# Lightning attention with a two-layer FFN on one core: step order from a list scheduler, transposes on the DMA queue, decay powers on V and the output

## The chip, the core and the metric

The kernel runs on one NeuronCore of a Trainium2 chip. The metric is the device time of one execution in microseconds (us). The span of a profile is about 1.8 us shorter than the device time of the same execution. A lower time is better. Each version was run several times on one chip, beside the kernel before; the median is given, with the lowest and the highest in brackets. A run is called slow when it is over 1.5% above the fastest of its kernel, and slow runs are left out of all comparisons.

In the profile PE is TensorE (matmul), PEld its weight loads, DVE is VectorE, ACT ScalarE, POOL GpSimd and SP SyncE. The letter q after an engine (SPq, POOLq) means its queue, in which it issues DMAs. L342 is line 342 of the kernel. POOL and GpSimd are the same engine in the text too.

## The reference

An attention with a decay per head is followed by an FFN. B=4, H=8, S=768, D=64; the FFN goes from 512 to 2048 columns and back.

```python
def _attn_ref(q, k, v, lam):                       # cut, and shortened to formulas
    for b in range(nb):                            # blocks of 64 positions
        intra = (q_b @ k_b.T * lam ** (i - j) for i >= j) @ v_b
        inter = (q_b * lam ** (pos + 1)) @ kv_state
        out[:, :, sl] = intra + inter
        kv_state = lam ** 64 * kv_state + (k_b * lam ** (63 - pos)).T @ v_b

def _moe_ref(x, w_in, w_out, alpha):
    h = x @ w_in
    s = np.sin(alpha * h)
    g = h + s * s / (alpha + 1e-09)
    return (g @ w_out).astype(np.float32)
# x = attention output, 3072 tokens x 512
```

## The kernel before

The attention is cut into 24 *units*, numbered 0 to 23. A unit is one batch, four heads and 256 positions, held as 128x512 elements each of Q, K and V. Four units give the input of one *group* of 512 tokens; there are six groups. For a unit the kernel loads Q, K and V (256 KB each), scales them to bf16, transposes Q and K, computes scores, masks them, and multiplies with V. FFN1 (times w_in, then sine and square) makes 16 tiles of 128x512 for a group; FFN2 (times w_out) makes four tiles of 512 columns from 16 matmuls each.

The decay is put into the operands: Q is multiplied by E = lam^pos and K by R = 1/E, V is only cast.

```python
    def scale_q(u, eng):
        ...
        eng.tensor_tensor(out=QL[:], in0=stage[u][0]...,
                          in1=E[:, :, hs].unsqueeze(3).to_broadcast([P, 2, HH, D]), op=ALU.mult)
    def scale_k(u, eng):   # the same with stage[u][1] and R
    def cast_v(u, eng):    # a copy to bf16
    def transposes(u, tag="s0", split=False):        # eight 128x128 transposes on PE
        ...
                    nc.tensor.transpose(out=pts[j][:, hp, par, :],
                                        in_=cast[u, key][:, par, 2 * hp:2 * hp + 2, :],
                                        identity=iden[:])
        ...
            nc.scalar.copy(out=QT[:], in_=pt[:])
```

The order of all instructions on each engine is written by hand. Units 0 to 7 come first, with four filler matmuls of zeros after each; then FFN1 of group 0 and half of FFN1 of group 1; then steps of one kind, called `macro`:

```python
    busy(N0)                                     # 28 filler matmuls
    ...
    group(0, "hps")                              # units 0-3; busy(4) after each
    group(1, "hps")                              # units 4-7; w_in is issued at units 5-7
    ...
    alone(NFC, hook0, (V, A, V, A, G, A, V, G))  # FFN1 of group 0: squares on DVE, ACT, POOL
    alone(NPRE, hook1)                           # 8 tiles of FFN1 of group 1

    def macro(n, nf, mid=None, late=None):
        ...   # scores of unit n, output of unit n-1, state of unit n
        F1 = [ffn1(*f1q.pop(0), V) for _ in range(nf)]   # squares on DVE
        F2 = blocks(ffn2(*f2q.pop(0)), 4)
        for j in range(4):
            st = F1[j] if j < nf else []
            run(st[:-1])
            if j == 1 and n + 1 < NU:
                transposes(n + 1)                # on PE
            run(st[-1:])
            run(F2[j])
            ...
    for n in range(8, NU + 4):
        macro(n, 4 if n >= 12 else NFC // 4 - NPRE // 4, mid2, late2)
```

Of the kernel before, what the change touches and what calls it, by code (L numbers as in the profile page):

```python
# [12 lines left out]
ET = mybir.EngineType  # L14
# [3 lines left out]
def kernel(  # L18
# [24 lines left out]
    RING = 8  # L43
    WIN0 = 5
    GATE = 8
    N0 = 28
    NB = 4
    NPRE = 8
# [3 lines left out]
    wpool = ctx.enter_context(tc.tile_pool(name="wts", bufs=1))  # L52
    stagep = ctx.enter_context(tc.tile_pool(name="stage", bufs=RING))
    work = ctx.enter_context(tc.tile_pool(name="work", bufs=3))
    kvp = ctx.enter_context(tc.tile_pool(name="kv", bufs=2))
    xtp = ctx.enter_context(tc.tile_pool(name="xt", bufs=3))
    gbp = ctx.enter_context(tc.tile_pool(name="gb", bufs=3))
    mlps = ctx.enter_context(tc.tile_pool(name="mlps", bufs=3))
    outp = ctx.enter_context(tc.tile_pool(name="outp", bufs=3))
    PS = bass.MemoryType.PSUM  # L60
    ps = ctx.enter_context(tc.tile_pool(name="ps", bufs=1, space=PS))

    ctx.enter_context(tc.manual_schedule())


# [7 lines left out]
    BUFS = {"s0": 1, "s1": 1, "okv": 1, "hps": 3, "ops": 1}  # L73
    stage = {}

    def load(u, after=None):
        _, tp, b, _, hh = where(u)
        st = []
        for nm, src in (("q", q), ("k", k), ("v", v)):
            tl = stagep.tile([P, HH, 2, D], FP32, name=f"st_{nm}")  # L80
            ld = nc.sync.dma_start(  # L81
                out=tl[:].rearrange("p h two e -> p h (two e)"),
                in_=src[b, hh * HH:(hh + 1) * HH, tp * W:(tp + 1) * W, :]
                .rearrange("h (p two) e -> p h (two e)", two=2))
            if after is not None:
                tc.add_manual_dep(ld.ins, after.ins.name, mybir.DependencyInfo(
                    mybir.DependencyClass.Sync, mybir.DependencyReason.DATA))
                after = None
            st.append(tl)
        stage[u] = st  # L90

    zeros = consts.tile([P, 2 * P], BF16, name="zeros")
    nc.vector.memset(zeros[:], 0.0)
    warm = consts.tile([1, 1], FP32, name="warm")
    nc.vector.memset(warm[:], 0.0)  # L95
    nc.scalar.activation(out=warm[:], in_=warm[:], func=ACTF.Sin)
    lam_bc = consts.tile([P, H], FP32, name="lam_bc")
    nc.sync.dma_start(out=lam_bc[:], in_=lam.partition_broadcast(P))
    alpha_r = consts.tile([NFC, P], FP32, name="alpha_r")
    nc.scalar.dma_start(out=alpha_r[:], in_=moe_alpha.rearrange("(f p) -> f p", p=P))  # L100
    for u in range(8):
        load(u)

# [3 lines left out]
    for c in range(2):  # L107
        sl = slice(c * D, (c + 1) * D)
        nc.gpsimd.iota(out=pos[sl, :], pattern=[[0, 1]], base=1, channel_multiplier=2,
                       allow_small_or_imprecise_dtypes=True)  # L110
        nc.gpsimd.iota(out=jt[sl, :], pattern=[[1, 2]], base=0, channel_multiplier=2,
                       allow_small_or_imprecise_dtypes=True)
    it = consts.tile([P, 2, D], FP32, name="it")
    nc.gpsimd.iota(out=it[:], pattern=[[1, 2], [2, D]], base=0, channel_multiplier=0,
                   allow_small_or_imprecise_dtypes=True)
# [5 lines left out]
    nc.vector.tensor_tensor(  # L121
        out=mask[:], in0=it[:].rearrange("p two e -> p (two e)").unsqueeze(1)
        .to_broadcast([P, 2, 2 * D]),
        in1=jt[:].unsqueeze(2).to_broadcast([P, 2, 2 * D]), op=ALU.is_ge)
    E = consts.tile([P, 2, H], FP32, name="E")
    R = consts.tile([P, 2, H], FP32, name="R")
    nc.gpsimd.tensor_tensor(out=E[:, 0], in0=lam_bc[:], in1=pos[:].to_broadcast([P, H]),
                            op=ALU.pow)

    LT = consts.tile([P, H], FP32, name="LT")  # L130
    nc.vector.tensor_tensor(out=LT[:], in0=lam_bc[:], in1=lam_bc[:], op=ALU.mult)
    for i in range(6):
        nc.vector.tensor_tensor(out=LT[:], in0=LT[:], in1=LT[:], op=ALU.mult)
    nc.vector.tensor_tensor(out=E[:, 1], in0=E[:, 0], in1=lam_bc[:], op=ALU.mult)
    nc.vector.reciprocal(out=R[:], in_=E[:])
# [3 lines left out]
    w_in_sb = wpool.tile([P, NDC, DFF], BF16, name="w_in_sb")  # L139
    w_out_sb = wpool.tile([P, NFC, DM], BF16, name="w_out_sb")  # L140
    WCH = 4

    def load_w_in(j):
        w = DFF // WCH
        nc.gpsimd.dma_start(
            out=w_in_sb[:, :, j * w:(j + 1) * w],
            in_=moe_w_in[:, j * w:(j + 1) * w].rearrange("(c p) g -> p c g", p=P))

    def load_w_out(j):
        n = NFC // WCH  # L150
        nc.gpsimd.dma_start(
            out=w_out_sb[:, j * n:(j + 1) * n, :],
            in_=moe_w_out[j * n * P:(j + 1) * n * P, :].rearrange("(f p) d -> p f d", p=P))

    cast = {}

    def scale_q(u, eng):
        hh = where(u)[4]
        QL = work.tile([P, 2, HH, D], BF16, name="QL")
        hs = slice(hh * HH, (hh + 1) * HH)  # L160
        eng.tensor_tensor(out=QL[:], in0=stage[u][0][:].rearrange("p h two e -> p two h e"),  # L161
                          in1=E[:, :, hs].unsqueeze(3).to_broadcast([P, 2, HH, D]),
                          op=ALU.mult)
        cast[u, "q"] = QL

    def scale_k(u, eng):
        hh = where(u)[4]
        KD = work.tile([P, 2, HH, D], BF16, name="KD", bufs=4)
        hs = slice(hh * HH, (hh + 1) * HH)
        eng.tensor_tensor(out=KD[:], in0=stage[u][1][:].rearrange("p h two e -> p two h e"),  # L170
                          in1=R[:, :, hs].unsqueeze(3).to_broadcast([P, 2, HH, D]),
                          op=ALU.mult)
        cast[u, "k"] = KD

    def cast_v(u, eng):
        VB = work.tile([P, 2, HH, D], BF16, name="VB", bufs=4)
        v_in = stage[u][2][:].rearrange("p h two e -> p two h e")
        if eng is nc.scalar:
            nc.scalar.copy(out=VB[:], in_=v_in)  # L179
        else:  # L180
            eng.tensor_copy(out=VB[:], in_=v_in)
        cast[u, "v"] = VB

    qkt = {}

    def transposes(u, tag="s0", split=False):
        QT = work.tile([P, 2, 2, 2, P], BF16, name="QT")
        if split:
            pts = [ps.tile([P, 2, 2, P], BF16, name="pt", tag=tag, bufs=BUFS[tag])
                   for j in range(2)]  # L190
        else:
            pt = ps.tile([P, 2, 2, 2, P], BF16, name="pt", tag=tag, bufs=BUFS[tag])
            pts = [pt[:, 0], pt[:, 1]]
        for j, key in ((0, "q"), (1, "k")):
            for hp in range(2):
                for par in range(2):
                    nc.tensor.transpose(out=pts[j][:, hp, par, :],  # L197
                                        in_=cast[u, key][:, par, 2 * hp:2 * hp + 2, :],
                                        identity=iden[:])
        if split:  # L200
            nc.scalar.copy(out=QT[:, 1], in_=pts[1][:])  # L201
            nc.vector.tensor_copy(out=QT[:, 0], in_=pts[0][:])
        else:
            nc.scalar.copy(out=QT[:], in_=pt[:])  # L204
# [378 lines left out]
```

## Time and profile before

| | before |
|---|---|
| time in the first runs, before the change was run | 236.38 us, median of 3 (235.03 to 236.7) |
| first FFN1 matmul starts | 31.84 us |
| one steady step (a unit's attention, 4 tiles of FFN1, one of FFN2) | 8.37 us |
| PE idle from the first FFN1 matmul to the last matmul (31.84 to 229.7) | 7.4 us |

The next lines are from the page of the kernel before. Part 2 shows the busy share of each engine in 40 equal slices of the span, in tenths (9 is 90% or more). PEclk is the clock that the throttle granted PE, DMA the share of the DMA engines. Part 4 is the chain of waits: the work that ended last, followed backwards.

```profile
span 234.5 us, 5410 instructions
## 1 busy us (share of the span) xinstructions
PE 213.9 (91%) x2166; PEld 113.9 (49%) x2189; DVE 154.4 (66%) x261; ACT 131.6 (56%) x216; POOL 115.5 (49%) x182
...
PE   8687689968899999999999999999999999998991
...
PEclk9999999997999999999999999999999999999999
...
PE 71%; SPq 7%; DVE 6%; POOL 4%; issue 4%; ACT 4%; DMA 2%; POOLq 0%; ACTq 0%
```

PE is above 90% in nearly all slices from the twelfth on (about 65 us), and it makes 71% of the chain. The gain must come from less work on PE, or from an earlier start.

One steady step is the PE timeline of the kernel before (start us, duration, engine, line, operation, out<-in, form, count). A duration holds the modelled drain of the last matmul, so one reads steps from start to start:

```profile
129.62 1.03 PE L369 MATMUL ops<-w_out_sb,gall 128*128 128x512 bf16 x4
...
131.34 0.39 PE L197 MATMUL pt<-iden,QL 128*128 128x128 bf16 x4
131.57 0.39 PE L197 MATMUL pt<-iden,KD 128*128 128x128 bf16 x4
131.79 1.03 PE L369 MATMUL ops<-w_out_sb,gall 128*128 128x512 bf16 x4
...
137.99 0.81 PE L369 MATMUL ops<-w_out_sb,gall 128*128 128x512 bf16 x3
```

The step takes 137.99 - 129.62 = 8.37 us. The eight transposes of the next unit take 131.79 - 131.34 = 0.45 us of it, with nothing beside them on PE.

The largest single wait of PE after the first units is in the list of PE's waits in the kernel before (who waited, line, for whom: total us, times, longest):

```profile
PE pt L197 <- DVE gall L356: 2.9, 1, 2.9
```

The timelines show its cause. First DVE's, then GpSimd's, of the kernel before:

```profile
48.77 3.40 DVE L355 TENSOR_TENSOR s_1127<-s_1125 128x512 bf16<-128x512 bf16 x1
```

```profile
48.84 1.06 POOL L161 TENSOR_TENSOR QL<-st_q,E 128x512 bf16<-128x512 f32 x1
49.85 1.04 POOL L170 TENSOR_TENSOR KD<-st_k,R 128x512 bf16<-128x512 f32 x1
50.85 1.03 POOL L355 TENSOR_TENSOR s_1153<-s_1151 128x512 bf16<-128x512 bf16 x1
```

One square on DVE took 3.40 us and ended at 52.17 us, 0.3 us after the last of GpSimd's three operations; at 54.19 and 55.30 us, with GpSimd idle, the same square took 0.42 us. This is what the Trainium skill describes in "SBUF — State Buffer", Who interferes with whom: DVE's second read port is GpSimd's port, and it is an exclusive lock. The trace agrees here.

### The profile page before, as it was taken

To read this page: it belongs to the slowest core of one execution; us is meant where nothing else is said; L and a number is where in the kernel's file an instruction comes from. 1 tells how busy PE (TensorE), PEld (TensorE's weight loads), DVE (VectorE), ACT (ScalarE), POOL (GpSimd) and SP (SyncE) were. 2 spreads that over 40 slices of the span, in tenths; PEclk is the share of its full clock that TensorE was granted. 3 is DMA by queue.
4 is the path that set the end of the run, shared out by engine and by line. 5 is a ranking of instruction groups with operands and counts; after the bars stand their busy time and mean duration, and the time that the engine had idled before them with its cause. 6 is when DMAs were issued, how large, how long until landed. Compare 5 with 4: busy or idle time off the path is not lost.

```text
span 234.5 us, 5410 instructions
## 1 busy us (share of the span) xinstructions
PE 213.9 (91%) x2166; PEld 113.9 (49%) x2189; DVE 154.4 (66%) x261; ACT 131.6 (56%) x216; POOL 115.5 (49%) x182
## 2 busy tenths in 40 slices
PE   8687689968899999999999999999999999998991
PEld 5465544324455554555555455455455444443440
DVE  3887948997766556686686687677668756765000
ACT  2466669966755755665646656556565535453110
POOL 5568976980989997855854642651511000000000
PEclk9999999997999999999999999999999999999999
DMA  5999899999846555534633633621122022210333
GB/s 153 296 291 290 148 181 184 207 180 268 236 124 179 155 156 157 150 77 137 178 70 113 180 101 90 173 45 25 22 48 45 0 48 45 45 43 13 82 67 67
DMA packets 46281, 29.72 MB, mean 127 GB/s; under 512 B 2208, under 2 KB 43184, under 8 KB 46256
## 3 DMA queue, kind: packets, MB, share of 16 engines
q1 hardware_dynamic: 42000, 25.18, 41.8%
q0 software_dynamic: 4224, 4.19, 11.8%
q8 instruction: 17, 0.28, 0.5%
q14 instruction: 8, 0.07, 0.1%
q10 hardware_dynamic: 32, 0.01, 0.0%
HBM read 27.28 MB, written 6.29 MB: 143 GB/s over the span
## 4 chain that ended last, share of the span: by engine, by line
PE 71%; SPq 7%; DVE 6%; POOL 4%; issue 4%; ACT 4%; DMA 2%; POOLq 0%; ACTq 0%
PE ops L369 35%; PE hps L342 26%; SPq L81 7%; PE pt L197 3%; PE sp L219 2%; DMA st_k<-in_k_dram 2%; DVE gall L356 2%; PE okv L313 2%; PE okv L298 2%; DVE s_1127 L355 1%; DVE QL L161 1%; ACT xt L324 1%; PE okv L247 1%; ACT ob L376 1%; POOL KD L170 1%
## 5 line engine op out<-in xcount | busy, mean ns | idle before, releaser
L342 PE MATMUL hps<-xt,w_in_sb 128*128 128x512 bf16 x364 | 94.8, 383 | 3.1 <-ACT xt L324 1.2
L369 PE MATMUL ops<-w_out_sb,gall 128*128 128x512 bf16 x381 | 94.6, 379 | 0.9 <-ACT ob L376 0.7
L342 PEld LDWEIGHTS <-w_in_sb 128*128 128x128 bf16 x384 | 36.4, 99 | 44.7 <-issue 4.5
L369 PEld LDWEIGHTS <-gall 128*128 128x128 bf16 x384 | 36.9, 98 | 42.6 <-issue 1.0
L230 DVE TENSOR_TENSOR ST<-sp,mask 128x512 bf16<-128x512 f32 x48 | 30.8, 682 | 1.5 <-PE sp L219 1.2
L170 POOL TENSOR_TENSOR KD<-st_k,R 128x512 bf16<-128x512 f32 x24 | 26.4, 1099 | 5.7 <-DMA st_k<-in_k_dram 5.1
L204 ACT COPY QT<-pt 128x1024 bf16<-128x1024 bf16 x16 | 16.2, 1012 | 21.9 <-PE pt L197 21.9
L376 ACT COPY ob<-ops 128x512 f32<-128x512 f32 x24 | 14.0, 585 | 19.1 <-PE ops L369 19.1
L324 ACT CAST xt<-okv 128x512 bf16<-128x512 f32 x24 | 14.1, 587 | 6.1 <-PE okv L247 5.2
L161 POOL TENSOR_TENSOR QL<-st_q,E 128x512 bf16<-128x512 f32 x16 | 17.4, 1088 | 0.0
L197 PE MATMUL pt<-iden,QL 128*128 128x128 bf16 x96 | 9.6, 223 | 4.8 <-DVE gall L356 2.9
L197 PE MATMUL pt<-iden,KD 128*128 128x128 bf16 x96 | 9.6, 224 | 3.5 <-POOL KD L170 3.4
L197 PEld LDWEIGHTS <-QL 128*128 128x128 bf16 x96 | 6.8, 99 | 9.7 <-issue 4.1
L179 ACT CAST VB<-st_v 128x512 bf16<-128x512 f32 x14 | 8.6, 616 | 5.1 <-DMA st_v<-in_v_dram 5.1
L419 PE MATMUL bz<-zeros 128*128 128x256 bf16 x60 | 10.3, 326 | 1.1 <-DVE warm L95 1.1
L219 PE MATMUL sp<-QT 64*64 64x128 bf16 x384 | 9.9, 221 | 0.7 <-ACT QT L201 0.7
L313 PE MATMUL okv<-ST,VB 64*64 64x128 bf16 x384 | 9.8, 218 | 0.0
L197 PEld LDWEIGHTS <-KD 128*128 128x128 bf16 x96 | 6.3, 100 | 4.7 <-POOL KD L170 4.7
L161 DVE TENSOR_TENSOR QL<-st_q,E 128x512 bf16<-128x512 f32 x8 | 7.8, 970 | 1.0 <-DMA st_q<-in_q_dram 0.9
L419 PEld LDWEIGHTS <-zeros 128*128 128x128 bf16 x60 | 6.5, 117 | 2.7 <-DVE warm L95 1.1
L219 PEld LDWEIGHTS <-QT 64*64 64x64 bf16 x384 | 6.4, 106 | 2.9 <-ACT QT L201 0.8
L247 PE MATMUL okv<-VB,KD 64*64 64x64 bf16 x320 | 7.2, 193 | 0.3
(531 smaller groups left out, 316.5 us busy)
## 6 DMA issues: line engine op xcount, KB each, us to landing
st_q<-in_q_dram SPq DMA_DIRECT2D x24, 256.0 KB, 4.0
st_k<-in_k_dram SPq DMA_DIRECT2D x24, 256.0 KB, 4.6
st_v<-in_v_dram SPq DMA_DIRECT2D x24, 256.0 KB, 5.1
out_dram<-ob SPq DMA_DIRECT2D x48, 128.0 KB, 2.4
w_in_sb<-in_moe_w_in_dram POOLq DMA_DIRECT2D x4, 512.0 KB, 6.5
w_out_sb<-in_moe_w_out_dram POOLq DMA_DIRECT2D x4, 512.0 KB, 8.1
lam_bc<-in_lam_dram SPq DMA_DIRECT2D x1, 4.0 KB, 3.0
alpha_r<-in_moe_alpha_dram ACTq DMA_DIRECT2D x1, 8.0 KB, 2.9
```

The costliest lines, as they stand in the source:

```text
L81: ld = nc.sync.dma_start(out=tl[:].rearrange("p h two e -> p h (two e)"), in_=src[b, hh * HH:(hh + 1) * HH, tp * W:(tp + 1) * W, :] .rearr ...
L161: eng.tensor_tensor(out=QL[:], in0=stage[u][0][:].rearrange("p h two e -> p two h e"), in1=E[:, :, hs].unsqueeze(3).to_broadcast([P, 2, HH ...
L170: eng.tensor_tensor(out=KD[:], in0=stage[u][1][:].rearrange("p h two e -> p two h e"), in1=R[:, :, hs].unsqueeze(3).to_broadcast([P, 2, HH ...
L197: nc.tensor.transpose(out=pts[j][:, hp, par, :], in_=cast[u, key][:, par, 2 * hp:2 * hp + 2, :], identity=iden[:])
L204: nc.scalar.copy(out=QT[:], in_=pt[:])
L219: nc.tensor.matmul(out=sp[hd][half[c], par, hp, :], lhsT=QT[half[hd], 1, hp, par, half[c]], rhs=QT[half[hd], 0, hp, :, half[c]], start=Tru ...
L230: nc.vector.tensor_tensor(out=ST[:, hd], in0=sp[hd][:], in1=mask[:].unsqueeze(2).to_broadcast([P, 2, 2, P]), op=ALU.mult)
L324: nc.scalar.copy(out=xt[g][:, 2 * hh:2 * hh + 2, bb, :, :].rearrange("p hp c i -> p c hp i"), in_=okv[:, :, 0:2 * P].rearrange("p c (hp i) ...
L342: f1mm[g, f] = nc.tensor.matmul(out=hps, lhsT=w_in_sb[:, c, f * P:(f + 1) * P], rhs=xt[g][:, c].rearrange("p b c i -> p (b c i)"), start=( ...
L369: f2mm[:] = [nc.tensor.matmul(out=ops[:], lhsT=gall[g][:, f, m * P:(m + 1) * P], rhs=w_out_sb[:, f, :], start=(f == 0), stop=(f == NFC - 1))]
L376: nc.scalar.copy(out=ob[:], in_=ops[:])
L419: nc.tensor.matmul(out=bz[:], lhsT=zeros[:, :P], rhs=zeros[:], start=True, stop=True)
```

## The change

The intent is fourfold.

1. **Order.** The order of the steps on each engine no longer is written by hand. The kernel describes each operation with an assumed duration, a priority, what it needs and which buffers it takes. A list scheduler, run while the kernel is built, plays this through and emits the operations in the order in which they started in its play. The order is static on the chip. FFN1 of group 0 may now run between units 4 to 7, and FFN1 of group 1 is split by batch (matmuls of 256 columns) so that its first half may start two units earlier.
2. **Decay.** Q and K are only cast; V is multiplied by R, and the output by E while it is read from PSUM, on DVE.
3. **Weights.** w_in is issued after the units 2 and 3 have been scaled and not at the units 5 to 7.
4. **Transposes.** Units 8 to 23 are transposed by DMA, issued in SyncE's queue, where all loads and stores are issued too.

The squares also move: 87 of 112 to ACT, 25 to GpSimd, none to DVE. Fillers remain only at the very start.

```diff
+class Plan:
+    ENG = ("PE", "DVE", "ACT", "POOL", "SP")
+    RATE, DMA_LAT = 300e3, 2.0          # bytes per us, us: what the scheduler assumes of DMA
+    ...
+                act = [q for q in queue.values() if q and q[0][1] <= last + 1e-9]
+                ...
+                for q in act:           # two queues (SP, POOL) share the rate in equal parts
+                    q[0][2] -= step * self.RATE / len(act)
+                    if q[0][2] <= 1e-3:
+                        finish(q.pop(0)[0], last + step + self.DMA_LAT)
...
-    def scale_q(u, eng):  ...  op=ALU.mult   # by E
-    def scale_k(u, eng):  ...  op=ALU.mult   # by R
+    def cast(op, u, j):   ...  tensor_copy
+    def scale_v(op, u):   ...  op=ALU.mult   # by R
...
+    def turn_dma(op, u):
+        T[u, "qt"] = slot(op, work, "qt", [P, 2, 2, 2, P], BF16)
+        SY.dma_start_transpose(
+            out=T[u, "qt"][:].rearrange("p j par hp i -> p (j par hp) i"),
+            in_=T[u, "qk"][:].rearrange("p j par h e -> p (j par h e)"))
...
+    WG = (2, 2, 3, 3, 4, 5, 6, 7)       # the unit behind which a quarter of w_in, w_out is issued
+    GATE8 = 8                           # unit 8's first load waits for FFN1 tile 8 of group 0
+    HALVES = (1,)                       # FFN1 of group 1 by batch
+    def SQ(g, f, hb):
+        return ("ACT", "POOL") if g < 2 else (("POOL",) if f % 5 == 4 else ("ACT",))
...
+            oo = add(f"ld{u}{'qkv'[i]}", on("SP", 0.5), [gate], vtl, ...)   # a load: 0.5 us of SP
...
+            dt = add(f"dt{u}", on("SP", .1), [cq, ck], b4 - 150, lambda op: turn_dma(op, u),
+                     take=("qt",), give=((cq, "qk"),), lag=3.5)
...
-    busy(N0)
-    ...
-    for n in range(8, NU + 4):
-        macro(n, 4 if n >= 12 else NFC // 4 - NPRE // 4, mid2, late2)
+    for op in plan.run():
+        op.emit(op)
```

The numbers in `on` and `lag` are the scheduler's: a load holds SyncE for 0.5 us; a transpose holds SyncE for 0.1 us, takes no share of the rate, and is complete at a fixed 3.5 us after its issue.

## The prediction

> **What bounds the kernel now.** From about 62 us on TensorE; before that, dependencies. The chain of waits gives PE 71% of the span. In its list by time four 512-column matmuls advance it 0.86 us, 0.216 us each; all 768 need 165.9 us. The timeline of one steady step (129.8 to 138.15 us) shows 8.37 us: 6.9 FFN, 0.45 for eight transposes, 1.01 for attention matmuls. The first FFN matmul starts at 31.84 us. FFN plus 16 units at 1.46 us (23.4) would then end at 221; the last matmul ends at 229.7, so about 8.6 us are holes. They lie at 45-62 us: the waits show PE held 2.9 us by a DVE result, after a square on DVE that took 3.4 us while GpSimd ran three operations back to back (other squares take 0.4 to 1.3). The windows table has the clock at 0.68 in 52-56 us. This fits the Trainium skill ("SBUF — State Buffer", Who interferes with whom: two SBUF inputs on DVE against GpSimd reads; "TensorE: Matmul & The Clock Gate", What's actually happening: idle PE is throttled).
>
> **What changes.**
> 1. FFN1 of group 0 needs only units 0-3 and a quarter of w_in, and is interleaved with units 4-7. Before, unit 3's attention was done near 21 us; a w_in quarter lands 6.5 us after issue. I estimate the first FFN matmul at 20 us: 11.8 us earlier, but units 4-7 (about 1.35 us of PE each, 5.4) now come after it: net 6.4 us.
> 2. Units 8-23 are transposed by DMA, not PE: 16 x 0.45 = 7.2 us off PE, on the critical path, as PE is full there; 16 ACT evictions of 1.01 us vanish. DMA is 10-60% busy after 62 us, so the transposes should fit.
> 3. Decay powers leave Q and K: two GpSimd multiplies of 1.09 us become casts (0.61), V's cast becomes the multiply; the output eviction moves from ACT (0.59) to DVE (estimate 0.7, from the mask's 0.68). Off the critical path later.
> 4. Squares leave DVE for ACT (87) and GpSimd (25): the port conflict and the 2.9 us hole should go. ACT gets 5.7 us of work in a 7.9 us step.
>
> **Against it.** The early phase is tight. By the time unit 11 is needed, 17.8 MB must have been read (12 units of 0.786 MB, weights 8.4 MB); at the 290 GB/s that the page shows at 6-23 us this is about 62 us. ACT, DVE and PE each have 45-51 us of work in the 50 us from the first FFN matmul to group 2's FFN1. I expect 4-6 us of holes there.
>
> **Sum.** First FFN 20 + FFN 165.9 + units 4-7 5.4 + units 8-23 16 x 1.0 - 0.6 + holes 4.5 = 211; plus 4.8 for the last eviction and store, as now, = 216; times are 1.9 above the profile's span: **about 217 us, range 209 to 225.** Faster by over 2%: 0.96; within 2%: 0.03; slower by over 2%: 0.01.
>
> **What would show it.** First FFN1 matmul at 18-23 us. No PE transposes after unit 7; a steady step of 7.8-7.9 us. No 16-bit squares on DVE. PE gap-free from about 65 us. Holes in 20-65 us that end on DMA (w_out, inputs of units 8-11) or ACT.
>
> **What would make it wrong.** DMA transposes that take over 8 us each or block loads behind them in the in-order SyncE queue; a clock drop at 8-20 us, where filler matmuls between units are gone; ACT or GpSimd stalls of a static order early; w_in slowing unit 3's loads so that FFN1 starts after 25 us.

## The result, and the profile after

The change made the kernel slower: **253.84 us** (252.88 to 255.52, 4 runs) against 236.06 us (235.03 to 236.7, 4 runs). The ratio is 1.074, with a 95% interval of 1.069 to 1.080. Ratios are computed as the mean time of one kernel's fast runs over that of the other's of the same rounds, so they are not quite the ratio of the quoted medians.

The page after, in the same lines as before:

```profile
span 252.3 us, 5359 instructions
## 1 busy us (share of the span) xinstructions
PE 213.9 (85%) x2079; PEld 114.1 (45%) x2105; DVE 124.5 (49%) x219; ACT 149.4 (59%) x273; POOL 123.5 (49%) x207
...
PE   8856597985039699979898999999999999999992
...
PEclk9985559999858999999999999999999999999999
...
PE 57%; DMA 15%; POOL 11%; SPq 7%; DVE 3%; ACT 3%; issue 3%; POOLq 0%; ACTq 0%
```

Compare the two rows of PE. Before, it is full from slice 12. After, it is full only from slice 23 (about 140 us), with a hole in slices 11 and 12 (63 to 76 us), where PE is at 0 and 3 tenths. The clock is at half in slices 4 to 6. DMA and POOL, which had 6% of the chain together, now have 26%.

The steady step of after, once PE is full (PE timeline):

```profile
144.58 1.03 PE L525 MATMUL ops<-w_out_sb,gall 128*128 128x512 bf16 x4
...
150.62 0.39 PE L454 MATMUL okv<-qt,kvbd 128*128 128x128 bf16 x4
...
152.51 0.81 PE L525 MATMUL ops<-w_out_sb,gall 128*128 128x512 bf16 x3
```

It takes 152.51 - 144.58 = 7.93 us against 8.37, as predicted: the 0.45 us of transposes are gone. So the late part of the kernel is faster by what the prediction said, and the loss must lie before 140 us.

PE's time splits as follows, from the tables of busy time by stretch:

| us | prediction | after | before |
|---|---|---|---|
| first FFN1 matmul starts | 20 | 29.99 | 31.84 |
| PE busy from there to the last matmul | 186.7 | 193.85 | 190.42 |
| PE idle in the same stretch ("holes") | 4.5 | 23.55 | 7.44 |
| last eviction and store | 4.8 | 4.9 | 4.8 |

The second row of the prediction is 165.9 + 5.4 + 16 x 1.0 - 0.6. The busy time after is 7 us above it; 8.95 us of it ran at a clock of 0.64 and 6.50 us at 0.59 (next table), which by an estimate makes 8.95 x 0.36 + 6.50 x 0.41 = 5.9 us lost to the clock. No run tests this estimate as a whole, and e9 speaks against taking it for the only reason (see the end). The idle time is 19 us above it, and the start 10 us later.

The table of stretches of after (stretch, length, busy time of PE, PEld, DVE, ACT and POOL with the number of instructions, granted clock, DMA share, GB/s):

```profile
20.00:30.00 10.00, 5.22 (x99) 3.55 (x99) 4.41 (x9) 2.13 (x5) 2.95 (x4) 0.50 1.20 216
30.00:40.00 10.00, 8.95 (x96) 4.15 (x100) 4.87 (x8) 5.57 (x11) 6.70 (x10) 0.64 1.18 246
40.00:50.00 10.00, 9.15 (x119) 4.37 (x110) 7.99 (x13) 9.04 (x18) 8.79 (x16) 1.00 0.60 98
50.00:60.00 10.00, 7.61 (x55) 3.96 (x55) 6.07 (x10) 7.62 (x15) 8.86 (x15) 1.00 1.19 278
60.00:70.00 10.00, 2.07 (x16) 1.46 (x15) 2.65 (x6) 3.69 (x10) 4.39 (x8) 0.89 1.21 291
70.00:80.00 10.00, 6.50 (x102) 4.09 (x104) 2.35 (x5) 2.35 (x6) 3.56 (x7) 0.59 1.23 244
```

In 20 to 30 us the clock was 0.50. The Trainium skill ("TensorE: Matmul & The Clock Gate", What's actually happening) says that a clock gate passes only a part of the pulses when PE has been little busy, half of them in the cold state, and the trace agrees with the half.

What PE waited for in after, from its list of waits:

```profile
PE sp L379 <- DMA qt<-qk: 9.8, 1, 9.8
PE hps L497 <- DVE gall L516: 9.2, 10, 1.6
PE pt L356 <- ACT qk L338: 7.6, 5, 2.4
```

There are three losses, one to a line. Asked for by stretches of time, they belong to three places: of the 7.6 us 7.0 lie before 30 us, the 9.8 us are one wait at 63 us, and of the 9.2 us 6.5 lie in 80 to 140 us and 2.7 in 50 to 80.

**First, before 30 us.** PE waits for casts on ACT, and those wait for inputs, as ACT's list of waits in after says:

```profile
ACT qk L338 <- DMA st_q<-in_q_dram: 12.1, 6, 4.2
```

PE's timeline in after:

```profile
24.90 0.61 PE L356 MATMUL pt<-iden,qk 128*128 128x128 bf16 x4 [1.76 <-ACT qk L338]
...
28.26 0.61 PE L356 MATMUL pt<-iden,qk 128*128 128x128 bf16 x4 [2.40 <-ACT qk L338]
28.66 0.42 PE L454 MATMUL okv<-qt,kvbd 128*128 128x128 bf16 x2
29.02 0.64 PE L467 MATMUL okv<-sm,vb 64*64 64x128 bf16 x16
29.99 1.49 PE L497 MATMUL hps<-xt,w_in_sb 128*128 128x512 bf16 x3 [0.33 <-issue]
```

FFN1 of group 0 needs units 0 to 3 only. But in the static order the output of unit 4 and the transposes of unit 5 stand ahead of it, and those wait for inputs.

**Second, 63 to 73 us.** PE stands for 9.8 us before unit 8's scores, for the first DMA transpose. The timeline of SyncE's queue in after shows why (start, time of the issue in the queue):

```profile
47.28 0.37 SPq L324 DMA_DIRECT2D st_q<-in_q_dram  x1
...
67.02 0.78 SPq L324 DMA_DIRECT2D st_v<-in_v_dram  x1
67.91 2.54 SPq L368 DMA_TRANSPOSE qt<-qk  x1
```

Unit 8's first load is issued at 47.28 us, after the gate on FFN1 tile 8. In the emitted order 21 loads (units 8 to 14) stand before the first transpose. Each holds the queue for 0.4 to 1.8 us, the transpose goes out at 67.91, and PE goes on at 73.28. During 40 to 50 us DMA moved only 98 GB/s, because the gate held the queue; in the list of waits of SyncE's queue it is the line of L324 that waits for FFN1:

```profile
SPq L324 <- PE hps L497: 11.6, 1, 11.6
```

A wait in this in-order queue holds everything behind it. This fits what the Trainium skill says ("DMA: Bandwidth & Descriptors", Anatomy of one DMA — SWDGE (gpsimd) path, a section on GpSimd's queue): DMA engines wait for no semaphore, any wait happens on the issuing sequencer before dispatch. The trace agrees for SyncE's queue: the 11.6 us stand in its own list.

**Third, 80 to 140 us.** PE is at 17.46, 17.57 and 17.80 us of 20, in the three stretches of 20 us; GpSimd is at 18.48, 15.56 and 17.61. The larger part of the waits for `gall` lies here. The square of a tile, where it is on GpSimd, waits behind casts, V's multiply and the states. And GpSimd does not only work there, it also stands, as its list of waits in after says:

```profile
POOL kvbd L430 <- PE okv L454: 8.1, 5, 2.7
```

Before it writes a unit's second state (kvbd), GpSimd waits five times until PE has read the state that this one overwrites; 6.6 of the 8.1 us lie in 80 to 140 us. The emitted order, computed again from the kernel's code, shows why: for the five units 11 to 15 it puts the write before the step in which PE reads the old state. Everything behind it on GpSimd, squares too, is held. The scheduler's graph lacks this dependency; e13 adds it.

The scheduler's own play, which is computed when the kernel is built and is no measurement, had the first FFN1 matmul at 22.2 us, unit 8's transpose at 46.4 us and unit 8's step at 50.1 us. On the chip they came at 30.0, 67.9 and 73.3.

### The profile page after: what moved, and what is told of

Same layout as the page of the kernel before. It is cut to its first block, busy times and chain, and to the rows that moved or that the text cites. A ratio compares the mean times of both kernels' runs of the same rounds, so it can differ in the third digit from the quotient of the medians.

```text
span 252.3 us, 5359 instructions
## 1 busy us (share of the span) xinstructions
PE 213.9 (85%) x2079; PEld 114.1 (45%) x2105; DVE 124.5 (49%) x219; ACT 149.4 (59%) x273; POOL 123.5 (49%) x207
## 4 chain that ended last, share of the span: by engine, by line
PE 57%; DMA 15%; POOL 11%; SPq 7%; DVE 3%; ACT 3%; issue 3%; POOLq 0%; ACTq 0%
PE ops L525 29%; PE hps L497 24%; DMA st_q<-in_q_dram 8%; SPq L324 7%; DMA st_k<-in_k_dram 5%; POOL vb L346 3%; POOL qk L340 2%; DVE gall L516 2%; DMA qt<-qk 2%; POOL s L513 2%; POOL kvbd L430 2%; PE sp L379 2%; POOL kvs L444 1%; PE okv L454 1%; ACT s L504 1%
## 5 line engine op out<-in xcount | busy, mean ns | idle before, releaser
L516 DVE SCALAR_TENSOR_TENSOR gall<-s,r_sb,hps 128x512 bf16<-128x512 bf16 (+1 forms) x112 | 73.4, 669 | 83.4 <-ACT s L511 51.2
L497 PE MATMUL hps<-xt,w_in_sb 128*128 128x512 bf16 (+1 forms) x431 | 100.3, 355 | 11.2 <-DVE gall L516 9.2
L504 ACT ACTIVATE s<-hps,alpha_sb 128x512 bf16<-128x512 f32 (+1 forms) x112 | 69.2, 625 | 54.6 <-PE hps L497 53.2
L511 ACT ACTIVATE s<-s 128x512 bf16<-128x512 bf16 (+1 forms) x87 | 49.1, 568 | 2.4
L513 POOL TENSOR_TENSOR s<-s 128x512 bf16<-128x512 bf16 (+1 forms) x25 | 23.0, 921 | 40.8 <-ACT s L504 40.7
L388 DVE TENSOR_TENSOR sm<-sp,mask 128x512 bf16<-128x512 f32 x48 | 32.7, 683 | 15.4 <-PE sp L379 15.3
L346 POOL TENSOR_TENSOR vb<-st_v,R 128x512 bf16<-128x512 f32 x24 | 24.9, 1043 | 9.4 <-DMA st_v<-in_v_dram 6.5
L427 POOL TENSOR_TENSOR kvx<-kva,kvs 128x128 f32<-128x128 f32 x32 | 14.6, 456 | 28.5 <-ACT kva L412 28.4
L430 POOL TENSOR_TENSOR kvbd<-kvx,LBD 128x256 bf16<-128x256 f32 x32 | 19.6, 613 | 10.2 <-PE okv L454 8.1
L484 DVE TENSOR_TENSOR xt<-okv,ET 128x512 bf16<-128x512 f32 x24 | 16.4, 683 | 1.9 <-PE okv L467 1.9
```

Source lines behind the costliest of these rows:

```text
L346: ENGINE[op.eng].tensor_tensor(out=T[u, "vb"][:], in0=T[u, "v"][:].rearrange("p h two e -> p two h e"), in1=R[:, :, hs].unsqueeze(3).to_br ...
L388: V.tensor_tensor(out=T[u, "sm"][:, hd], in0=T[u, "sp"][hd][:], in1=mask[:].unsqueeze(2).to_broadcast([P, 2, 2, P]), op=ALU.mult)
L430: G.tensor_tensor(out=bd[:], in0=X.unsqueeze(2).to_broadcast([P, 2, 2, D]), in1=LBD[:, hs, :].unsqueeze(3).to_broadcast([P, 2, 2, D]), op= ...
L497: op.ins = nc.tensor.matmul(out=op.tile[:, cols], lhsT=w_in_sb[:, c, f * P:(f + 1) * P], rhs=xt[g][:, c].rearrange("p b c i -> p (b c i)") ...
L504: A.activation(out=op.tile[:, cols], in_=mm.tile[:, cols], func=ACTF.Sin, scale=alpha_sb[:, f:f + 1])
L511: A.activation(out=op.tile[:, cols], in_=s1, func=ACTF.Square)
```

## The experiments

Five theories were on the table, named by letters in the expectations:

- **A**: the weights, now loaded early, take bandwidth from the inputs of units 3 to 7.
- **B**: the DMA transposes stand behind the loads in SyncE's queue.
- **C**: GpSimd carries too much in 80 to 140 us; the squares there are the part that can go elsewhere.
- **D**: the clock falls in the first 40 us, because the fillers between the units are gone.
- **E**: the root of these is the scheduler's picture of DMA: it emits an order that is good under its assumptions and bad on the chip.

Their rivals were that the DMA transposes themselves are the cost, and that any static order from this scheduler loses. Each set of runs was timed beside the kernel before on its own chip, whose medians were 236.57, 235.78, 236.39 and 236.18 us in the four sets. All results were correct unless it is said otherwise.

### e2: transposes ahead of loads in SyncE's queue (theory B)

```diff
-    for op in plan.run():
+    order = plan.run()
+    for u in range(11, NU):        # loads of unit u go behind the transpose of unit u - 3
+        if order.index(ld[u][0]) < order.index(names[f"dt{u - 3}"]):
+            ... move the three loads to just behind it
+    for op in order:
```

> Edit: the SyncE queue issues the loads of units 11 and later only behind the DMA transpose of the unit three before; every other engine keeps its order. Theory B (queue order: the first transpose stood behind 21 loads, issued at 67.9 us, and TensorE waited 9.8 us for it): that wait falls under 2 us and the time falls by 8 to 12 us, to about 242 to 246. Rival A (DMA is simply short of bandwidth, so what is moved forward in the queue delays something else by as much): the time stays within 3 us of 253.8. Rival C (GpSimd work is the limit from 80 to 136 us): the hole goes but TensorE meets GpSimd sooner, and 2 to 5 us are gained.

Measured: 242.62 us (242.1 to 243.84), ratio 1.028 [1.023, 1.032]. That is 11 us less than after, from moving loads in one queue. SyncE's timeline in this run:

```profile
55.39 0.73 SPq L324 DMA_DIRECT2D st_v<-in_v_dram  x1
56.30 2.73 SPq L368 DMA_TRANSPOSE qt<-qk  x1
```

The first transpose goes out at 56.30 instead of 67.91, and the 9.8 us wait is gone from PE's list. Theory B holds. The kernel is still slower than before.

One thing in this profile was not edited: the first FFN1 matmul starts at 26.36 us, not 29.99, though the moved loads are all issued after 47 us. Kernels whose emitted order is the same up to there fall into two kinds: 26.4 us in e2 and e13 and 26.9 in e12, but 29.8 to 30.2 in after, e3, e4, e6, e8 and e14. In e2 SyncE's queue was one load further when, at 17 us, the issue of a load began to take 3 us and more; why is not known. The lead is lost again at once: unit 8's first load is issued at 48.02 us in e2 and 48.78 in e13, against 47.28 in after. A difference of this size in the start is therefore no evidence for an edit.

### e3: unit 8's load released by the first FFN1 tile

```diff
-   lambda op, ...: load(op, u, i, gate if i == 0 and u == 8 else None)
+   lambda op, ...: load(op, u, i, f1_mm[0, 0, None] if i == 0 and u == 8 else None)
```

> Edit: the load of unit 8 waits for the first FFN1 block (30 us) instead of the ninth (46.8 us); no order changes. The DMA engines moved only 86 to 165 GB/s at 38-50 us. If that idle stretch is part of the loss, unit 8 lands about 10 us earlier, the first transpose is issued near 57 us instead of 67.9, the 9.8 us wait shrinks to under 3 us and the time is 242 to 247. If the DMA is short of bandwidth throughout (A), the weights just come later and the time stays within 3 us of 253.8.

Measured: 248.49 us (247.44 to 249.91), ratio 1.052. DMA moved 260 GB/s in 40 to 50 us instead of 98, the first transpose went out at 62.5, and the wait shrank from 9.8 to 5.9 us. It gained 5 us, a little less than expected, and the wait did not fall under 3 us. The lateness of the gate is a part of B, not all of it.

### e4: squares of groups 1 to 3 from GpSimd to ACT (theory C)

```diff
+    for op in order:
+        if op.name starts with "sq_1", "sq_2" or "sq_3" and op.eng == "POOL":
+            op.eng = "ACT"
```

> Edit: the squares of groups 1 to 3 that the schedule gave to GpSimd run on ACT, at the same places. Theory C (GpSimd, busy 52 of 60 us at 80-140 us, holds TensorE there): TensorE rises from 52.8 busy us in that stretch to about 58 of 60 us and the time falls by 4 to 7 us, to 247 to 250. If GpSimd is not the limit, the time stays within 2 us of 253.8. The 9.8 us wait before 73 us stays in both cases.

Measured: 248.93 us (247.98 to 250.3), ratio 1.055. The stretches of this run, in the columns as above:

```profile
100.00:120.00 20.00, 19.89 (x198) 11.05 (x199) 12.46 (x22) 15.94 (x33) 17.24 (x34) 1.00 0.71 173
120.00:140.00 20.00, 19.84 (x217) 10.33 (x219) 12.43 (x19) 15.07 (x27) 14.14 (x24) 1.00 0.76 139
```

PE is full in 100 to 140 us, where it had 17.57 and 17.80, and 5 us are won. To take squares off GpSimd cures this stretch; the wait for the transpose stays at 9.6 us. It does not show that GpSimd had too much work: e13 gains the same with all of these squares left to ACT and GpSimd as the scheduler likes.

### e5: a quarter of the weights (theory A; wrong result)

```diff
-   lhsT=w_in_sb[:, c, f * P:(f + 1) * P]
+   lhsT=w_in_sb[:, c, (f % 4) * P:(f % 4 + 1) * P]
-   rhs=w_out_sb[:, f, :]
+   rhs=w_out_sb[:, f % 4, :]
-   lambda op, j=j: load_w_in(op, j)                    # and load_w_out
+   lambda op, j=j: load_w_in(op, j) if j == 0 else None
```

> Wrong result on purpose: only the first quarter of each weight is loaded and used four times over, with the same matmuls in the same order; this takes 6.3 MB of DMA reads out of the first 60 us. Theory A (the early phase is short of DMA bandwidth, the weights beside the first inputs starve units 5 to 7): the first FFN1 matmul starts at 20 to 24 us instead of 30, the clock stays above 0.9 at 20-40 us, unit 8 is in before it is needed and the time falls by 18 us or more, to 236 or less. Rival (the static order and the engines set the pace): the first FFN1 stays after 27 us and the time above 247.

Measured: 246.05 us (244.44 to 246.74), ratio 1.040; the result is wrong, as intended (relative error 1.72). With 6.3 MB less to read the first FFN1 matmul starts at 27.4 us, not 30 (within the spread told under e2), and the wait for the transpose stays at 9.0 us. But unit 8's first load is released at 41.19 us, not 47.28, and unit 8's scores come at 64.94, not 73.28. Eight us are won by taking away three quarters of the weight traffic, which fits neither expectation well. So the weights' bytes cost time before 47 us, but no bandwidth saving brings the predicted 20 us. A falls as the main cause.

### e6: fillers before the transposes of units 2 to 7 (theory D)

```diff
     def turn_pe(op, u, j):
+        if 2 <= u < NT:
+            bz = bank(op, "f", [P, 2 * P], FP32, "bz")
+            for _ in range(3):
+                nc.tensor.matmul(out=bz[:], lhsT=zeros[:, :P], rhs=zeros[:], start=True, stop=True)
```

> Edit: three matmuls on zeros before each transposition of units 2 to 7, as filler for TensorE; nothing else. Theory D (the granted clock, 0.5 from 15 to 36 us because the fillers between units are gone, delays the first FFN1 and slows what follows): clock at 15-36 us above 0.9, first FFN1 at 26 to 28 us instead of 30, time down by 4 to 8 us, to 246 to 250. If the inputs of units 5 to 7 set the pace there, the clock recovers but the time falls by less than 3 us.

Measured: 253.79 us (253.61 to 254.56), ratio 1.077: nothing. The clock rose to 1.00 in 10 to 20 and 0.81 in 20 to 30 us (0.83 and 0.50 without fillers), and PE still waited 5.6 us for the same casts. Up to 30 us inputs set the pace, and theory D falls for that stretch. In 30 to 40 us the fillers did not bring the clock back (0.68 against 0.64), so what the slow clock costs there is not tested.

### e8: e2, e3, e4 and e6 together

> Edit: the changed kernel with four repairs at once: transposes ahead of later loads, unit 8 gated on the first FFN1 block, squares of groups 1 to 3 off GpSimd, fillers before the transposes of units 2 to 7. If the losses are apart in time and add up (11 + at most 5, of which part is the same wait, + 5 + 5), the time is 228 to 233, better than both kernels. If they hide one another, 234 to 240.

Measured: 236.21 us (235.8 to 236.56), ratio 1.001 [1.000, 1.003]: the loss is gone, the gain has not come. The gains of the four single edits add up to 21.5 us, together they are 17.6, the second of the two expected outcomes. PE has 19.9 us of 20 in each stretch from 80 us on, and there is no wait for transposes. The first FFN1 matmul is still at 30.23 us, and PE still waits 6.6 us for casts of late inputs. In 20 to 30 us PE is busy 4.86 us, as in after (5.22). So the two late losses are cured, and what is left lies before 80 us: in 30 to 80 us PE is busy 42.2 us, where e9, below, has 46.2.

### e1 and e12: units 8 to 23 transposed on PE again, the rest as after

```diff
-   dt = add(f"dt{u}", on("SP", .1), [cq, ck], b4 - 150, lambda op: turn_dma(op, u), ...)
-   qt, hold = [dt], dt
+   tq = add(f"tq{u}", on("PE", .22), [cq], b4 - 6, lambda op: turn_pe(op, u, 0), ...)
+   ...                                          # e0, tk, e1, as for units 0-7
+   qt, hold = [e0, e1], tq
```

> Edit: units 8 to 23 are transposed on TensorE again (two transposes of Q and K halves, evicted by ACT and DVE), the rest of the change stays; the list scheduler places them, so the order moves a little. If the DMA transposes cost the time (theory B), the 9.8 us wait for the first of them goes, its clock dip too, and 16 x 0.45 = 7.2 us of TensorE work comes back: 246 to 250. If the DMA transposes were only unlucky in their place and the rest is lost elsewhere, the steady step after 140 us is 8.4 us instead of 7.93. If they had nothing to do with it: 261.

Measured: 260.39 us median, with fast runs from 258.05 to 260.42, ratio 1.101. One execution of the four took 451.46 us, and the profile fell into it. The expectation of 246 to 250 is missed. For a usable profile it was run once more:

> The same kernel as e1, once more for a profile of its usual state, as that of e1 fell into an execution of 451 us. If transposes on TensorE leave unit 8 waiting for its loads (gated at the ninth FFN1 block) and not for a transpose, TensorE has a wait of 5 us or more on ACT or a load near 60 us, and a steady step of 8.4 us. Time 258 to 261.

Measured: 261.57 us (one run, state unknown). PE waits 14.4 us for `gall`, 13.1 of them in 80 to 140 us, the longest time 5.1 us, and has 14.72, 16.22 and 15.89 us of 20 in the stretches from 80 to 140 us, while neither ACT nor GpSimd is full. So the expected wait near 60 us is missed. From 140 us on PE is full, with a step of 8.55 us. GpSimd's wait for the old state, 8.1 us in after, is 19.5 us here (five times, up to 5.6). The scheduler, given other operations, made another order, in which the missing dependency costs more. This suggests that the DMA transposes are not the disease, since without them the kernel is slower still, but it can't show it (e7 does); and it shows that a rerun of the scheduler changes far more than the one thing that was edited, so undoing a part through it is a poor experiment.

### e7 and e11: the kernel before with DMA transposes alone

e7 keeps the hand-written order and transposes units 10 to 23 by DMA. The transpose of unit n+1 is issued at the start of step n, ahead of the loads of that step.

```diff
+    def transposes_dma(u):
+        QT = work.tile([P, 2, 2, 2, P], BF16, name="QT")
+        nc.sync.dma_start_transpose(
+            out=QT[:].rearrange("p j par hp i -> p (j par hp) i"),
+            in_=cast[u, "qk"][:].rearrange("p j par h e -> p (j par h e)"))
...
+        if 10 <= n + 1 < NU:
+            transposes_dma(n + 1)       # before mid(n), which issues the loads
...
-            if j == 1 and n + 1 < NU:
+            if j == 1 and n + 1 < 10:
                 transposes(n + 1)
```

> Edit: the kernel before, with units 10 to 23 transposed by DMA, issued a step ahead of use and ahead of the next loads in the queue; nothing else of the change. If the term of the prediction was right (0.45 us of TensorE per unit on the critical path), 14 x 0.45 = 6.3 us are gained: 229 to 231.5. If DMA transposes are bad for this kernel in themselves, the time is 236 or more, with TensorE waiting on their landing.

Measured: **229.82 us** (229.59 to 230.06), ratio 0.975 [0.973, 0.976]. The gain is 235.78 - 229.82 = 6.0 us, against 14 x 0.45 = 6.3 expected. The prediction's second term stands, and the rival that transposes themselves cost time falls.

e11 does the same from unit 8 on:

> Edit: the kernel before with units 8 to 23, not only 10 to 23, transposed by DMA. The first transpose (unit 8) is issued near 51 us, ahead of the loads of units 9 and 10. If DMA transposes are harmless early too as long as they stand ahead of the loads, another 0.9 us goes: 228.5 to 229.5. If the busy DMA of that phase makes them late, TensorE waits for them and the time is 231 or more.

Measured: 230.70 us (229.71 to 232.3), ratio 0.980 [0.973, 0.986]. The further 0.9 us did not come: PE waits 4.7 us in two places for the first transposes, which are issued when SyncE's queue is still full of loads.

### e9: other DMA numbers for the scheduler (theory E)

The scheduler is told what the trace shows: a load holds SyncE for 0.85 us, a transpose for 1.25 us, and the transpose's 256 KB take their turn in the queue; when both queues are busy, SyncE's gets one third of the rate and GpSimd's two thirds.

```diff
+   part = {id(q): (1 if len(act) < 2 else 1 / 3 if q is queue["SP"] else 2 / 3) for q in act}
-   q[0][2] -= step * self.RATE / len(act)
+   q[0][2] -= step * self.RATE * part[id(q)]
-   oo = add(f"ld{u}{'qkv'[i]}", on("SP", 0.5), ...)
+   oo = add(f"ld{u}{'qkv'[i]}", on("SP", 0.85), ...)
-   dt = add(f"dt{u}", on("SP", .1), [cq, ck], b4 - 150, ..., lag=3.5)
+   dt = add(f"dt{u}", on("SP", 1.25), [cq, ck], b4 - 201, ..., lag=.5, size=P * 1024 * 2)
+   if u in d1s and u >= NT:            # in flush(): the second state of unit u is
+       d1s[u].after.append(io)         # made after the step that reads the one before it
```

The thirds come from this view of after, the DMA queues in 17 to 36 us (packets, MB, share of 16 engines' time), when both queues always had work:

```profile
q0 software_dynamic: 2568, 2.55, 79.2%
q1 hardware_dynamic: 3477, 1.73, 40.0%
```

GpSimd's queue (q0) had twice the engine time of SyncE's (q1). The two shares add up to 119%, so they are times of packets that overlap and not parts of a whole; in bytes landed it is 2.55 to 1.73 MB, one and a half to one.

> Edit: the changed kernel's list scheduler gets the DMA behaviour that the trace shows, and nothing else: a load takes SyncE 0.85 us to issue (was 0.5), a transpose 1.25 us and 256 KB of the queue in its turn (was 0.1 us and a fixed 3.5 us), and while both queues run the GpSimd queue gets two thirds of the rate (was half). Theory E (the loss is the static order made from a wrong DMA model): the order places the first attention step of unit 8 later and fills TensorE before it; the 9.8 us wait goes and the time is 240 to 245, without any repair by hand. Rival (the order can't help, the bytes come too late): above 250.

One thing in this expectation is not right: the edit holds more than those numbers. It also has the last two lines of the diff, the dependency that was missing in the scheduler's graph and that the order of after breaks for units 11 to 15, and it raises the priority of transposes above that of loads (b4 - 201). Runs e13 to e15 take these apart.

Measured: **230.04 us** (229.54 to 230.57), ratio 0.976 [0.970, 0.983]. That is 23.8 us less than after and better than expected. The interval reaches just past the 2% line, so that it is faster is sure, and that it is so by over 2% is not. The stretches of e9, as above:

```profile
60.00:70.00 10.00, 9.45 (x62) 5.94 (x61) 4.42 (x10) 7.58 (x19) 8.45 (x12) 1.00 1.22 259
70.00:80.00 10.00, 9.94 (x96) 6.42 (x95) 5.74 (x12) 8.37 (x21) 4.36 (x8) 1.00 1.16 230
...
24.60:223.40 198.80, 193.51 (x1796) 99.61 (x1792) 109.44 (x174) 134.97 (x252) 108.06 (x179) 0.99 0.67 141
```

PE has 9.45 and 9.94 us of 10 where it had 2.07 and 6.50. From the first FFN1 matmul, now at 24.6, to the last it is idle for 198.80 - 193.51 = 5.3 us, against 23.55 in after. The start is 5.4 us earlier and the idle time 18.3 us less, which together make the 23.7 us. The timeline of PE in e9 shows what happened to unit 8:

```profile
75.40 1.03 PE L526 MATMUL ops<-w_out_sb,gall 128*128 128x512 bf16 x4
76.35 0.42 PE L380 MATMUL sp<-qt 64*64 64x128 bf16 x16
```

Unit 8's scores come at 76.35 us, *later* than in after (73.28), and its transpose still goes out behind 19 loads, at 60.89 us. But the order now has FFN work before it, and PE does not stand still. The loss in after was not that the transpose was late. It was that the order had put too little before unit 8's step, because the scheduler believed that the transpose would be there. The emitted orders, computed again from the code, have 20.5 tiles of FFN1 and one of the 96 blocks of four FFN2 matmuls before that step in after, 30 and 14 in e9. e14 below shows the same with nothing else changed.

### e10: e9 with the weights issued late

```diff
-    WG = (2, 2, 3, 3, 4, 5, 6, 7)
+    WG = (5, 5, 6, 7, 7, 7, 7, 7)
```

> Edit: as e9, and w_in is issued behind the V scaling of units 5 to 7, w_out behind that of unit 7, about as in the kernel before, instead of units 2 to 7. If the weights beside the first inputs cost time (theory A), units 5 to 7 come 5 to 8 us earlier, the first FFN1 stays near 30 us but with unit 7's attention done, and the time is 3 us or more below e9. If the place of the weights doesn't matter, it is within 2 us of e9.

Measured: 230.84 us median; its three fast runs are 230.18 to 230.88, ratio 0.979 [0.972, 0.985]. The profile fell into a slow run (234.1) and is read only for the order: its first FFN1 matmul is at 33.7 us instead of 24.6. The time is within 1 us of e9's. With a suitable order it does not matter whether FFN1 starts at 25 us between units 4 to 7 or at 34 us after them, because those units must be done in either case. So the start alone is worth little, as far as a start read from a slow run shows it, and moving the weights forward is worth nothing that these runs resolve.

### e13, e14, e15: e9 taken apart

e13 is after with only the missing dependency (the last two lines of e9's diff). e14 adds the transpose's numbers to e13, without the raised priority. e15 adds the load's 0.85 us and the shares of the queues to e13, and leaves the transpose's numbers as they were.

> Edit: the changed kernel with one more ordering edge in the scheduler (the second state tile of a unit is made only after the attention step that reads the old one), which e9 to e15 all contain; it permutes some steps after 54 us of the plan. If e9 gained through the corrected DMA numbers, this alone leaves the time at 250 to 257 and the wait of 9 us or more for the first transpose. If e9 gained by the accident of another order, it is below 245.

> Edit: as e13, and in the scheduler a transpose takes 1.25 us of SyncE and waits its turn behind the loads with 256 KB (was 0.1 us and a landing 3.5 us after, whatever was queued). Theory E1 (the wrong landing time of the transposes is what put unit 8's step where TensorE had to wait): the scheduler puts the first step of unit 8 about 22 us later in its plan, the wait of 9.8 us goes, and the time is 232 to 240, most of the 24 us of e9; the first FFN1 stays at 30 us. If the loads' numbers are what matters, above 248.

> Edit: as e13, and in the scheduler a load takes 0.85 us of SyncE and the two DMA queues share one to two (was 0.5 us and half and half); transposes as in the change. Theory E2 (the early order, unit 5 ahead of the first FFN1, came from loads believed too fast): the first FFN1 comes at 24 to 26 us as in e9 instead of 30, a gain of 4 to 7 us, but the wait for the first transpose stays: 246 to 250. If it accounts for most of e9, below 240.

| run | us, median (lowest to highest) | ratio | first FFN1 | wait for the first transpose |
|---|---|---|---|---|
| after | 253.84 (252.88 to 255.52) | 1.074 | 30.0 | 9.8 |
| e13: dependency | 247.95 (247.42 to 249.34) | 1.051 | 26.4 | 9.4 |
| e14: e13 + transpose's numbers | 238.92 (238.24 to 239.17) | 1.011 | 29.9 | none |
| e15: e13 + load's numbers | 238.22 (238.16 to 238.41) | 1.009 | 24.8 | 8.5 |
| e9: both, and the priority | 230.04 (229.54 to 230.57) | 0.976 | 24.6 | none |

The column of first FFN1 is no effect of the edits between after, e13 and e14 (see e2). The transpose's numbers are worth 247.95 - 238.92 = 9.0 us, and the wait for the first transpose is what they take away. That transpose itself is as late in e14 as in after (67.91):

```profile
67.93 2.54 SPq L368 DMA_TRANSPOSE qt<-qk  x1
```

The load's numbers are worth 247.95 - 238.22 = 9.7 us, more than expected: this run puts FFN1 ahead of unit 4's output and unit 5's transposes, releases unit 8's first load at 39.45 us (48.78 in e13) and scores unit 8 at 67.92 (73.17), has PE full from 80 us on (19.75, 19.89 and 19.84 of 20), and keeps the 8.5 us wait:

```profile
PE sp L380 <- DMA qt<-qk: 8.5, 1, 8.5
PE hps L498 <- DVE gall L517: 2.0, 5, 1.0
```

The two parts add up: 247.95 - 9.0 - 9.7 = 229.2, and e9, which has both, measured 230.04. The raised priority is thus not needed to explain e9. e13 missed its expectation: it gained 253.84 - 247.95 = 5.9 us, with PE at 19.89 and 19.84 in 100 to 140 us. That is about what e4 won from the same stretch with other means. What the dependency took away is in the lists of waits: GpSimd's five waits for the old state, 8.1 us, are gone in e13, and PE's waits for `gall` fell from 9.2 to 2.6 us, though the new order gives GpSimd three squares more. So e9's gain has three parts: 5.9 us from the dependency, 9.0 and 9.7 from the DMA numbers.

### e16: e9 with squares of groups 2 to 5 on ACT or DVE

```diff
-   return ("ACT", "POOL") if g < 2 else (("POOL",) if f % 5 == 4 else ("ACT",))
+   return ("ACT", "POOL") if g < 2 else ("ACT", "DVE")
```

> Edit: as e9, and the squares of groups 2 to 5 may go to ACT or DVE, whichever the scheduler finds free, instead of one in five to GpSimd. In e9 TensorE is 38.6 of 40 us busy at 80-120 us, with GpSimd 19.5 of 20 in its second half. If GpSimd holds it there, 1 to 2 us are gained: 228 to 229.5. If the holes of e9 are all before 60 us, the time stays within 1 us of 230; if 16-bit squares on DVE and GpSimd block each other as in the kernel before, it is 231 or more.

Measured: **229.52 us** (229.34 to 229.68), ratio 0.971 [0.967, 0.976]. This is the best time, level with e7's 229.82, and faster than before by over 2%. It is within 1 us of e9, the second of the expected outcomes: in 80 to 120 us PE is busy 37.9 us, not more than e9's 38.6, so GpSimd did not hold it there. The half microsecond between e16 and e9 is not resolved, as their intervals overlap.

## Why the prediction was wrong

The prediction said 217 us and faster with a chance of 0.96. It is 253.84. Point by point:

- **"four 512-column matmuls advance it 0.86 us", "8.37 us"; transposes "7.2 us off PE, on the critical path".** Right. The steady step went to 7.93 us, inside the predicted 7.8 to 7.9 to a few hundredths, and the hand-ordered kernel with only this change gained 6.0 us (e7).
- **"I estimate the first FFN matmul at 20 us".** Wrong: 29.99 us. The estimate took it that the matmul starts when its own inputs are there. In a static order it starts when everything ahead of it in the order is done, and that was unit 4's output and unit 5's transposes, which waited for inputs. The same order started at 26.4 us in e2 and e13, without gain. With other DMA numbers in the scheduler it started at 24.6 to 24.8 us (e9, e15). Of the 11.8 us that the prediction saw in an early start, little is there to be had: with the start at 33.7 us e10 lost 0.8 us to e9.
- **"I expect 4-6 us of holes there" (4.5 in the sum).** This is the term that failed most: 23.55 us of idle PE, and by the estimate above about 6 us of a slow clock. 9.8 us of it is the wait for the first DMA transpose (B: e2, e14), and about 10 us are waits for FFN1's evictions, 6.5 of them in the stretch where GpSimd had squares beside casts and states and stood for the old state of five units (e4, e13).
- **"DMA is 10-60% busy after 62 us, so the transposes should fit".** True of the share and beside the point. The first transposes fall in 47 to 75 us, when 21 loads were queued ahead of them. What decided was the place in an in-order queue. The prediction named this among its risks ("block loads behind them in the in-order SyncE queue"), with the direction reversed: it was the loads that held the transposes.
- **"Squares leave DVE ... the 2.9 us hole should go".** That hole went, and ten smaller waits for the same tile came, 9.2 us in all, because the squares on GpSimd waited behind other work, and behind a write that waited for PE (e13). DVE lost 30 us of busy time that was no limit; e16 gives squares back to DVE and loses nothing.
- **"PE gap-free from about 65 us".** From about 140 us.
- **"a clock drop at 8-20 us, where filler matmuls between units are gone".** It happened (0.83 in 10 to 20, 0.50 in 20 to 30 us) and was not a cause there: fillers restored the clock to 1.00 and 0.81 and not the time (e6). The slow clock of 30 to 40 us (0.64) is not tested.

The common step under these failures is that the prediction costed the change as a sum of operations and took the scheduler's order for a good one. The order was good only for the scheduler's own DMA, and its graph lacked a dependency. With its numbers nearer to the trace and the dependency added (e9), and no operation of the change removed, the same kernel takes 230.04 us. This is shown, and so are the three parts of it (e13, e14, e15).

Even then the range of 209 to 225 us is not reached. In e9 the busy PE time of 193.51 us, the start at 24.6 us and 5.3 us of holes add up to 223.4 us; the prediction had 186.7, 20 and 4.5. So the busy term was too small as well, by 6.8 us, and the clock is not the main part of it here: only the 5.00 busy us of 25 to 30 us ran slow (0.59), by the same estimate 2.1 us. The rest is not explained.

What stays open is why kernels with the same early order start FFN1 at 26.4 or at 30 us, where the rest of the busy time comes from, and what the single execution of 451 us in e1 was.

## What to carry to other kernels

A static order from a scheduler is only as good as the durations it is given, and here in-order engines turned its mistakes into idle time: compare the scheduler's assumed start of a few operations with the first trace, DMAs first, before judging anything else about the change. Give it every dependency that the reuse of a buffer makes: a missing one was no error here but 5.9 us. In a queue that issues both loads and DMA transposes, put the transpose ahead of loads that are not yet needed, or plan for it to be late. Test the parts of a bundled change on the old kernel where the order stays put; here the transposes alone gave 2.5% there, when the bundle lost 7.4%.

## What the Trainium skill lacked or had wrong

- "Advanced Engine Details and Errata", X-Bar Transpose (TRN2), says that "TRN2 transpose DMAs are as fast as regular DMAs". From issue to landing this agrees: in 84 to 126 us of after 256 KB took 3.4 us in the median, against 3.4 to 4.2 us for loads of the same size. It says nothing of the issuing queue: a transpose held SyncE's queue for 1.23 to 2.55 us, a load mostly for 0.4 to 0.9 us. The section also expects about 90% of a plain copy's bandwidth. An estimate from e7 is lower: its queue time rose from 41.8% of 234.5 us to 52.3% of 227.8 us with 14 transposes, so each took about 1.5 us of all 16 engines; the loads and stores of the kernel before, 25.18 MB in the 41.8%, took 1.02 us per 256 KB, so by this estimate a transpose had 68% of their rate.
- "DMA: Bandwidth & Descriptors", Issuing engines are not separate DMA queues, says that DMAs from all engines run on the same 16 DMA engines and interleave. The trace agrees, but the page gives no figure for how they share: with both queues full in 17 to 36 us, GpSimd's had 79.2% and SyncE's 40.0% of the engines' time, two to one, and 2.55 and 1.73 MB landed.
- No page that was read says that an issue itself takes longer when the queue is full of transfers: a load's issue took SyncE from 0.37 to 3.9 us in one run (after), with the median at 0.64 to 0.75 us. A scheduler that assumes 0.5 us has 21 loads out in 10.5 us; here they took 20.6 us (47.28 to 67.91).
